# Value products in two pieces instead of three, under a new order of all operations (fused attention and token mixing, one core)

## The chip, the cores and the metric

The kernel runs on one core of a Trainium2 chip. The metric is the device time of one execution in microseconds (us), the median of three runs. Each execution computes the whole problem: eight batches of attention with eight heads each, and behind each batch a mixing stage.

## What is computed

```python
scores = matmul(q, k^T) / sqrt(64)               # (8, 8, 576, 576)
scores = where(scores >= max(scores) - tau, scores, -1e9)
attn = exp(scores - max) ; attn = attn / (sum(attn) + 1e-9)
x = matmul(attn, v)                              # heads side by side: (8, 576, 512)
theta = x @ w_theta
zr, zi = x * cos(theta), x * sin(theta)
u = x + w_tok_r @ zr + w_tok_i @ zi              # mixing along the sequence
out = u + relu(u @ w_ch)
```

All inputs are float32. The large products are made of three products each of rounded high and low parts.

## The kernel before, in words

The work goes by pairs of heads: 8 batches x 4 pairs = 32 pairs, numbered 0 to 31. Everything is kept transposed, with channels on the partitions.

One pair has five units of scores (`unit`, line 743), the first four of 128 queries for each of two heads, the last of 64 queries of both. A unit is one run of score products on TensorE (line 759), then on VectorE an eviction with the row maximum (line 780) and a small addition (line 790), on ScalarE two activations that apply the threshold and the exponential (lines 804 and 811), and on VectorE a transpose in blocks of 32 x 32 (lines 823 and 825) into the tile `a`. There is one buffer of `a` (`n_a` is 1), so the transposes of a pair wait until the value products of the pair before have read it.

When all transposes of a pair are there, `values` (line 829) multiplies with v. These are 18 x 4 x 2 = 288 small products of 32 rows, 64 columns and 144 streamed elements (line 840), which use the array as eight tiles of 32 x 64. Every product is one weight load and one matmul, so a pair has 576 TensorE instructions there. They add up in four banks of PSUM. The 18 steps are cut into `parts` pieces of equal size, each one operation of the plan, and the operations between two pieces may be anything the order puts there:

```python
parts = AT["parts"]
for i in range(parts):
    c0, c1 = 18 * i // parts, 18 * (i + 1) // parts
    pe(..., lambda c0=c0, c1=c1: products(c0, c1), key + A("vs", n) * i, (a, v), (ps,),
       32 * (c1 - c0), mode="w", hold=[x])
```

After them ScalarE copies the four banks to `xT` (lines 853 and 856), and `divide` (line 860) divides by the row sums. After the fourth pair of a batch, `mixture` (line 913) adds the mixing stage: products with w_theta and w_ch (line 948), sine and cosine (lines 1044 to 1051), transposes on TensorE (line 1091) and the products along the sequence (line 1136). All of these are products of 128 rows, 128 columns and 128 to 288 elements, and they are spread over the next batch's four pairs, so that TensorE has them beside the attention. The first pairs have the conversion of the weights beside them (`convert`, line 552).

The order is written out. Every operation of every engine is recorded in a plan with a number; `Plan.run` then issues all of them in one list, `ORDER` (line 144), which holds the differences of the numbers. Each engine works through its own operations in the order of that list, and waits where data or a buffer is not ready. `PLACES` says which buffer or bank each operation uses. Queues of DMAs are issued by SyncE (SP) in the same list.

```python
for word in ORDER.split():
    step, times = (word + "*1").split("*")[:2]
    for _ in range(int(times)):
        n += int(step)
        self.ops[n].fn()
```

Followed through these numbers, the three pieces of a pair stand directly behind one another on TensorE in all 32 pairs: 288 small products in a row, with 126 to 486 other TensorE instructions between one pair's and the next pair's.

Of the kernel before, what the change touches and what calls it, by code (L numbers as in the profile page):

```python
# [64 lines left out]
        "0112101021012012011200120102102010210212021200210221021201021012012100"  # L65
    ),
    "xl": (
        "010320010120001230101201310230123021310231023102301320123201301230123102302130213"
    ),
    "xh": (  # L70
        "01120310032003230210310102310201230113021301230123120310232103102310230123012301230132102310230213"
    ),
    "rb": (
        "010101010010010101010000000000100000001000000100"
    ),
    "bank": (
        "77756745564674655645670000000060000006000000500000064776467564577657653457545746667654564757000000300000"
        "05000000500000056447567455327563476564577677547476760000006000000500000060000005754676754234763654645475"
        "66647554677600000050000006000000500000075475766544237426655665673447656476570000004000000400000050000006"
        "57465764553275656475476534547657466700000070000007000000700000066547566745324536574764567676574567470000"  # L80
        "00700000060000005000000456467547653624754765564577756745656700000060000007000000600007542354736525626275"
        "464625734576735467"
    ),
    "z": (
        "1021212012001200102010201200120010201200101"
    ),
    "rawq": (
        "01100110110101010010110101011110"
    ),
    "q": (  # L90
        "0123012301230123012301230123012301230123012301230123012301230123"
# [11 lines left out]
        "01320123103120132013202103130120132101230120103102110201231032031020132121031012032011032012102130112302"  # L103
        "13210123011201230023102103203123021103202310100210312102301201102302120103201012012131032013233210231300"
        "12301201201010203210310322012302031320101201020110210012310231102321012103201120"
    ),
    "nm": (
        "01010101012010201010200100120101010100100101010012010100101010010010120110101012100100101201010100101001"
        "00101210100010010101020011011201001010010010120101001010"
    ),  # L110
    "s2": (
        "01010010101001201120010100120010212010121001001212102101021201120012011001201012010120101010020100120101"
        "20110120102010210112001021011200112101021010211020101021"
    ),
    "rows": (
        "00010001010100101010101010010100"
# [5 lines left out]
        "01234560123405612340516203452160"  # L122
# [8 lines left out]
        "0102011001320120012010230123010201010123010101230123012001230231"  # L131
    ),
    "zl4": (
        "0123203101320123012332010123201301230123012010230123012301230231"
    ),
    "zh1": (
        "01010101010101000000000100010101"
    ),
    "zl1": (
        "01100101011001100101010100100101"  # L140
# [1172 lines left out]
```

## Time and profile before

| what | value |
|---|---|
| median of three runs | 979.58 us (978.79 to 985.16) |
| profiled execution, its own time | 993.05 us |
| span of the profiled execution | 991.3 us |
| TensorE busy | 885.7 us (89%), 14632 matmuls |
| VectorE busy | 714.8 us (72%) |
| ScalarE busy | 701.1 us (71%) |
| GpSimd busy | 311.9 us (31%) |
| mean granted TensorE clock | 0.96 of full speed |

In the profile, PE is TensorE's matmuls and PEld its weight loads, which run beside them; DVE is VectorE, ACT is ScalarE, POOL is GpSimd, SP is SyncE. "Idle before" a group is the time for which the engine had nothing running just before, with what ended it; "issue" there means that the engine waited for nothing that the profile shows. A matmul in the profile lasts until its modelled end, and the next one starts before that.

### The profile page before, as it was taken

Reading aid. Unit: us, or ns where it says so; the run is one execution under the profiler, and the core shown is the slowest. Engines: PE = TensorE matmul, PEld = TensorE weight load, DVE = VectorE, ACT = ScalarE, POOL = GpSimd, SP = SyncE. Lnnn points to the kernel's source line nnn. Section 1 sums busy time; section 2 is a strip of 40 time slices with the busy share of each in tenths; the row PEclk is TensorE's granted clock in tenths of the full one; section 3 lists DMA queues with packets and bytes.
Section 4 is the critical chain, followed back from the end, with each engine's and each line's share of the span. In section 5 each row is a group of like instructions: output and inputs, shape, how many; then the busy total and the mean of one; then the engine's idle time right before and its main releaser. Section 6 shows DMA issues by size and latency. Waiting matters only on the chain.

```text
span 991.3 us, 34023 instructions
## 1 busy us (share of the span) xinstructions
PE 885.7 (89%) x14632; PEld 799.8 (81%) x14632; DVE 714.8 (72%) x1598; ACT 701.1 (71%) x1406; POOL 311.9 (31%) x390
## 2 busy tenths in 40 slices
PE   5678789988999999988899999998999898998898
PEld 3556678877898888978798888887898887998898
DVE  7889879866778877657777777686777676775343
ACT  6778789755997569845978569865787558974450
POOL 1223425312344325332334323422145221621201
PEclk9788899989999999989999999999999999999899
DMA  6446453444613354223603344315342343224301
GB/s 240 127 146 200 147 172 119 127 154 136 205 61 121 125 165 163 86 88 93 236 9 142 121 162 150 119 42 174 116 152 76 108 151 120 87 95 134 114 34 69
DMA packets 62375, 126.15 MB, mean 127 GB/s; under 512 B 22512, under 2 KB 31632, under 8 KB 58128
## 3 DMA queue, kind: packets, MB, share of 16 engines
q1 hardware_dynamic: 62080, 123.97, 37.7%
q8 instruction: 115, 1.88, 0.8%
q14 instruction: 36, 0.29, 0.1%
q10 hardware_dynamic: 144, 0.00, 0.0%
HBM read 110.17 MB, written 13.78 MB: 125 GB/s over the span
## 4 chain that ended last, share of the span: by engine, by line
PE 69%; DVE 17%; issue 9%; ACT 3%; POOL 0%; DMA 0%; DVEq 0%; ACTq 0%; POOLq 0%
PE banks_ps__66 L1136 20%; PE banks_ps__66 L840 17%; PE banks_ps__66 L948 15%; PE banks_ps__66 L759 12%; DVE sc L780 7%; DVE a L823 4%; PE banks_ps__66 L1091 3%; DVE nm L790 1%; PE banks_ps__66 L634 1%; ACT sc L804 1%; ACT s L811 1%; DVE xl L530 1%; PE banks_ps__66 L871 1%; DVE xT L1197 0%; DVE a L825 0%
## 5 line engine op out<-in xcount | busy, mean ns | idle before, releaser
L804 ACT ACTIVATE sc<-sc,nm 128x576 f32<-128x576 f32 x288 | 217.4, 772 | 88.8 <-DVE nm L790 88.4
L823 DVE STREAM_TRANSPOSE a<-s 128x576 f32<-128x576 f32 x256 | 190.0, 759 | 123.1 <-PE banks_ps__66 L840 110.3
L840 PE MATMUL banks_ps__66<-a,v 32*64 32x144 f32 x9216 | 175.1, 296 | 62.8 <-issue 61.6
L811 ACT ACTIVATE s<-sc,small 128x576 f32<-128x576 f32 x288 | 223.0, 775 | 7.1 <-DVE a L823 2.4
L840 PEld LDWEIGHTS banks_ps__66<-a,v 32*64 32x64 f32 x9216 | 155.6, 136 | 79.0 <-issue 73.2
L780 DVE TENSOR_SCALAR_CACHE_REDUCE sc<-banks_ps__66 128x576 f32<-128x576 f32 x261 | 187.1, 744 | 44.0 <-PE banks_ps__66 L759 41.5
L759 PE MATMUL banks_ps__66<-k,q 64*128 64x288 f32 (+1 forms) x1728 | 180.7, 322 | 24.6 <-DVE sc L780 16.5
L759 PEld LDWEIGHTS banks_ps__66<-k,q 64*128 64x128 f32 (+1 forms) x1728 | 142.8, 197 | 51.3 <-DVE sc L780 26.5
L948 PE MATMUL banks_ps__66<-xh,wm 128*128 128x288 f32 x1024 | 173.2, 309 | 3.4 <-issue 2.8
L1136 PE MATMUL banks_ps__66<-wt_h,zh 128*128 128x288 f32 x576 | 163.0, 307 | 2.1 <-ACT zh L1097 1.7
L1136 PE MATMUL banks_ps__66<-wt_l,zh 128*128 128x288 f32 x576 | 161.6, 303 | 0.0
L948 PEld LDWEIGHTS banks_ps__66<-xh,wm 128*128 128x128 f32 x1024 | 147.8, 194 | 14.6 <-issue 11.9
L1066 POOL TENSOR_TENSOR z<-z,xT 128x288 f32<-128x288 f32 x112 | 91.3, 847 | 105.3 <-ACT z L1047 105.3
L1136 PEld LDWEIGHTS banks_ps__66<-wt_h,zh 128*128 128x128 f32 x576 | 109.5, 191 | 5.0 <-ACT zh L1097 2.1
L1136 PEld LDWEIGHTS banks_ps__66<-wt_l,zh 128*128 128x128 f32 x576 | 109.7, 191 | 2.1 <-issue 1.9
L530 POOL TENSOR_TENSOR xl<-xT,xh 128x288 fp32r<-128x288 f32 x78 | 65.1, 855 | 131.1 <-ACT xh L907 74.4
L1136 PE MATMUL banks_ps__66<-wt_h,zl 128*128 128x288 f32 x576 | 97.8, 305 | 1.1 <-DVE zl L1116 1.1
L530 POOL TENSOR_TENSOR k<-rawk,k 128x288 fp32r<-128x288 f32 x62 | 53.3, 872 | 135.9 <-ACT k L724 56.1
L948 PE MATMUL banks_ps__66<-xl,wm 128*128 128x288 f32 x512 | 92.5, 303 | 0.7 <-POOL xl L530 0.6
L853 ACT COPY xT<-banks_ps__66 128x512 f32<-128x512 f32 x32 | 18.8, 586 | 103.8 <-PE banks_ps__66 L840 103.8
L1136 PEld LDWEIGHTS banks_ps__66<-wt_h,zl 128*128 128x128 f32 x576 | 82.5, 190 | 4.3 <-issue 2.7
L894 POOL TENSOR_TENSOR xT<-xT,rb 128x288 f32<-128x288 f32 x48 | 39.4, 836 | 139.0 <-ACT xT L853 87.3
(78 smaller groups left out, 1068.1 us busy)
## 6 DMA issues: line engine op xcount, KB each, us to landing
v<-in_vp_dram SPq DMA_DIRECT2D x32, 1152.0 KB
wm<-wm_dram SPq DMA_DIRECT2D x64, 512.0 KB
rawq<-in_qT_dram SPq DMA_DIRECT2D x31, 320.0 KB
rawk<-in_kT_dram SPq DMA_DIRECT2D x31, 288.0 KB
out_dram<-xT SPq DMA_DIRECT2D x31, 288.0 KB
rb<-sums_dram SPq DMA_DIRECT2D x64, 128.0 KB
z<-in_w_tok_dram SPq DMA_DIRECT2D x9, 576.0 KB
wm_dram<-rb SPq DMA_DIRECT2D x16, 256.0 KB
```

The costliest lines, as they stand in the source:

```text
L530: eng.tensor_tensor(out=out()[:, c0:c1], in0=in0()[:, c0:c1], in1=in1()[:, c0:c1], op=ALU.subtract)
L759: nc.tensor.matmul(ps()[:, 2 * j + h, :HS], q[a]()[r, i * P : (i + 1) * P], k[c]()[r, h * HS : (h + 1) * HS], start=(x == 0), stop=(x == 2),)
L780: lambda j=j, sc=sc, scaled=scaled: nc.vector.tensor_scalar(out=sc().rearrange("p (a b) -> p a b", a=2), in0=ps()[:, 2 * j : 2 * j + 2, :H ...
L804: lambda j=j, sc=sc: nc.scalar.activation(out=sc(), in_=sc(), func=AF.Prelu, bias=nm()[:, 2 + j : 3 + j], scale=-1.0, alpha=STEEP),
L811: lambda j=j, sc=sc, total=total, weights=weights: nc.scalar.activation(out=weights(), in_=keys(sc()), func=AF.Exp, bias=back, accum_out=p ...
L823: nc.vector.transpose(out=a()[:, :, j, 32 * i : 32 * i + 32], in_=src.rearrange("p (c q) -> p c q", q=32))
L840: nc.tensor.matmul(ps()[64 * h : 64 * h + 64, b, :w], v()[r, c, h, :], a()[r, c, h, :], start=(c == 0), stop=(c == 17))
L894: eng.tensor_tensor(out=x()[:, r], in0=x()[:, r], in1=rc()[:, r], op=ALU.mult)
L948: nc.tensor.matmul(ps[h]()[:, :HS], wm()[:, a, c, :], parts[c][bb]()[:, h * HS : (h + 1) * HS], start=first and n == 0, stop=final and n = ...
L1066: eng.tensor_tensor(out=zi, in0=zi, in1=x[m]()[:, c0:c1], op=ALU.mult)
L1091: nc.tensor.transpose(out=tp()[:, i * P : (i + 1) * P], in_=z()[:, c : c + P], identity=ident)
L1136: nc.tensor.matmul(ps()[:, :HS], zz[c][lo]()[:, zz[c][2]], w[:, c, hs], start=(q + n == 0), stop=(q + n == len(work) - 1),)
```

## The change

`parts` becomes 2: each pair's value products are two operations of 144 small products (288 TensorE instructions each) in place of three of 96. The plan has 4369 operations in place of 4401, as many instructions on each engine's data path as before (14632 matmuls), and a new `ORDER` and new `PLACES`. All other numbers of `AT`, the buffers and the functions stay.

```diff
-    "px0": 2, "pu0": 2, "lc": 1, "ka": 4, "vq": 1, "pd": 3, "vs": -2.88, "parts": 3, "ab": 0, "sq": 3, "acc": 0.1,
+    "px0": 2, "pu0": 2, "lc": 1, "ka": 4, "vq": 1, "pd": 3, "vs": -2.88, "parts": 2, "ab": 0, "sq": 3, "acc": 0.1,
...
 ORDER = (
-    "176 -176 177 1 1 -9 10 1 -10 1*4 8 1 1 44 1 -44 45 -230 1*3 189 2 -1 -7 2 -184 183 44 -36 37 2 -1 -44 9 -2 1 5 "
...
+    "176 -176 179 -2 1 2 -10 1 1 9 -8 1 1 54 -46 2 -1 46 -44 1 44 -38 1 -5 6 1 36 1 1 -46 3 -1 13 2 -1 31 -38 -5 7 "
...
```

Followed through the new numbers, the two pieces of a pair no longer stand together. Between them stand, in the order of the pairs, 10, 16, 18, 24, 114, 50, 44, 40, 40, 54, 44, 40, 40, 68, 44, 50, 40, 54, 44, 40, 48, 52, 42, 40, 32, 120, 56, 48, 50, 54, 44 and 48 other TensorE instructions (median 44). From pair 4 on all of them belong to products and transposes of 128 rows of the mixing stage, to the one transpose of `divide`, or (pairs 5 and 6) to the conversion of w_ch. In pairs 0 to 3 they are the transpose of `divide` and products of the conversion. On the other engines the positions of most operations have moved as well.

## Rows read from the trace of the kernel before

**Rows 1.** The page's part 1: busy time, share of the span, instructions of each engine.
```profile
PE 885.7 (89%) x14632; PEld 799.8 (81%) x14632; DVE 714.8 (72%) x1598; ACT 701.1 (71%) x1406; POOL 311.9 (31%) x390
```
**Rows 2.** The page's part 4: the chain that ended last, by engine.
```profile
PE 69%; DVE 17%; issue 9%; ACT 3%; POOL 0%; DMA 0%; DVEq 0%; ACTq 0%; POOLq 0%
```
**Rows 3.** Waits of PE: what it waited for, us in total, times, longest.
```profile
PE banks_ps__66 L840 <- issue: 61.6, 37, 4.0
PE banks_ps__66 L759 <- DVE sc L780: 16.5, 18, 1.8
PE banks_ps__66 L759 <- DVE q L705: 6.1, 1, 6.1
PE banks_ps__66 L871 <- DVE rows L867: 4.0, 4, 2.1
```
**Rows 4.** Timeline of PE around one pair: start, length, what, [idle before].
```profile
629.74 0.69 PE L1136 MATMUL banks_ps__66<-wt_h,zl 128*128 128x288 f32 x4
630.36 2.51 PE L840 MATMUL banks_ps__66<-a,v 32*64 32x144 f32 x144
633.57 2.27 PE L840 MATMUL banks_ps__66<-a,v 32*64 32x144 f32 x128 [0.70 <-issue]
637.04 0.51 PE L840 MATMUL banks_ps__66<-a,v 32*64 32x144 f32 x16 [1.20 <-issue]
```
**Rows 5.** Timeline of PE around another pair, and the products behind it.
```profile
318.86 3.00 PE L840 MATMUL banks_ps__66<-a,v 32*64 32x144 f32 x176
322.73 2.02 PE L840 MATMUL banks_ps__66<-a,v 32*64 32x144 f32 x112 [0.87 <-issue]
324.68 0.40 PE L1136 MATMUL banks_ps__66<-wt_h,zh 128*128 128x288 f32 x1
...
325.18 0.30 PE L1136 MATMUL banks_ps__66<-wt_l,zh 128*128 128x288 f32 x1
325.31 0.29 PE L1136 MATMUL banks_ps__66<-wt_h,zh 128*128 128x288 f32 x1
```
**Rows 6.** The page's part 3: instruction packets by queue.
```profile
q8 instruction: 115, 1.88, 0.8%
```
**Rows 7.** Timeline of PE's weight loads around the pair of rows 5.
```profile
318.86 2.73 PEld L840 LDWEIGHTS banks_ps__66<-a,v 32*64 32x64 f32 x176 [0.16 <-issue]
...
324.68 0.19 PEld L1136 LDWEIGHTS banks_ps__66<-wt_h,zh 128*128 128x128 f32 x1 [0.20 <-issue]
```
**Rows 8.** Line 840 by itself: duration in ns, min/median/max.
```profile
L840 PE MATMUL banks_ps__66<-a,v x9216: 277/281/498, 29.0 to 920.6; 32*64 32x144 f32 x197
L840 PEldq EVENT_SEMAPHORE  x31: 51/51/51, 53.6 to 909.5; - x31
```
**Rows 9.** Waits of VectorE and ScalarE for the value products.
```profile
DVE a L823 <- PE banks_ps__66 L840: 110.3, 22, 9.1
ACT xT L853 <- PE banks_ps__66 L840: 103.8, 31, 11.4
```
**Rows 10.** Stretches: length, busy PE PEld DVE ACT POOL, PEclk, DMA share, GB/s.
```profile
30.00:180.00 150.00, 125.08 (x2048) 104.04 (x2035) 129.11 (x264) 121.03 (x247) 54.30 (x69) 0.89 0.48 152
180.00:620.00 440.00, 405.49 (x7150) 369.56 (x7149) 322.88 (x737) 323.71 (x654) 145.43 (x176) 0.98 0.39 131
620.00:910.00 290.00, 266.70 (x4579) 243.98 (x4578) 206.33 (x474) 212.10 (x424) 95.84 (x118) 0.98 0.34 113
```
**Rows 11.** Timeline of VectorE around the pair of rows 5.
```profile
320.27 0.55 DVE L696 TENSOR_SCALAR rawq<-rawq,small 128x640 f32<-128x640 f32 x1
324.88 0.78 DVE L823 STREAM_TRANSPOSE a<-s 128x576 f32<-128x576 f32 x1 [4.07 <-PE banks_ps__66 L840]
```

More of the change, by code (lines that the diff above doesn't have):

```diff
@@ L64 @@
     "wm": (
-        "0112101021012012011200120102102010210212021200210221021201021012012100"
+        "0101201220220101200012012001201201201201022100121010210210012012011200"
     ),
     "xl": (
-        "010320010120001230101201310230123021310231023102301320123201301230123102302130213"
+        "012102012001010231010120303120123201301230213012310230123301210232013102310232013"
     ),
     "xh": (
-        "01120310032003230210310102310201230113021301230123120310232103102310230123012301230132102310230213"
+        "01203121013003013120120213201323010103210310230123210301230213012312030123102310231023102320131023"
@@ L72 @@
     ),
     "rb": (
-        "010101010010010101010000000000100000001000000100"
+        "010101010001010101010000001000100000011101010100"
     ),
     "bank": (
-        "77756745564674655645670000000060000006000000500000064776467564577657653457545746667654564757000000300000"
-        "05000000500000056447567455327563476564577677547476760000006000000500000060000005754676754234763654645475"
-        "66647554677600000050000006000000500000075475766544237426655665673447656476570000004000000400000050000006"
@@ L80 @@
-        "57465764553275656475476534547657466700000070000007000000700000066547566745324536574764567676574567470000"
-        "00700000060000005000000456467547653624754765564577756745656700000060000007000000600007542354736525626275"
-        "464625734576735467"
+        "67765674454565747576560000000070000007000000700000074567545744744475677457667547667576477675000000600000"
+        "06000000600000056547646757456744754665674747677564570000005000000700000060000004765476576574567747655567"
+        "74476545675600000040000007000000600000077564757467556437476556747564674775670000006000000600000070000006"
@@ L83 @@
+        "65745576564654776746554766575647745600000040000004000000600000047456567465556774564574677546754765760000"
+        "00300000070000007000000576457675457467357456654767676476547600000060000006000000500005573273654727244354"
+        "663726656457766453"
     ),
     "z": (
-        "1021212012001200102010201200120010201200101"
+        "1201010212001200120012001200120012001200101"
     ),
     "rawq": (
-        "01100110110101010010110101011110"
+        "01011100110010100101101010100010"
@@ L89 @@
     ),
     "q": (
-        "0123012301230123012301230123012301230123012301230123012301230123"
+        "0123012301302103120312031203120312031203120312031201320123012301"
     ),
@@ L102 @@
     "sc": (
-        "01320123103120132013202103130120132101230120103102110201231032031020132121031012032011032012102130112302"
-        "13210123011201230023102103203123021103202310100210312102301201102302120103201012012131032013233210231300"
-        "12301201201010203210310322012302031320101201020110210012310231102321012103201120"
+        "10231032013201230132100231032101023031201230231202031012030112031021012020120123021032110213201230120310"
+        "13202130012303102130120321103201203012302130023103201320120312231020123012313210103202103121032031023102"
+        "31010230012301320132030123201301230130210230120301231123021031203121031321020310"
     ),
     "nm": (
-        "01010101012010201010200100120101010100100101010012010100101010010010120110101012100100101201010100101001"
-        "00101210100010010101020011011201001010010010120101001010"
+        "01010101010101020010100101001010101010100101010101201001001010001010012001010010100102010201010100101001"
+        "00102010010200100101001102100102001010010010120101010010"
     ),
     "s2": (
-        "01010010101001201120010100120010212010121001001212102101021201120012011001201012010120101010020100120101"
-        "20110120102010210112001021011200112101021010211020101021"
+        "01010010100101010010012101020201010100120112001001102010101010210001011020101102010100101010001100121010"
+        "10120210010011201001001102100101002001102012011001001102"
     ),
     "rows": (
-        "00010001010100101010101010010100"
+        "00100001001000101001010101000000"
     ),
@@ L121 @@
     "xT": (
-        "01234560123405612340516203452160"
+        "01234560321405632140536410253461"
     ),
@@ L130 @@
     "zh4": (
-        "0102011001320120012010230123010201010123010101230123012001230231"
+        "0120012001020132012301320102102001021023101001010102020101010101"
     ),
     "zl4": (
-        "0123203101320123012332010123201301230123012010230123012301230231"
+        "0123012001320132012301320132102001321023102301200123023101230120"
     ),
     "zh1": (
-        "01010101010101000000000100010101"
+        "01010010000100100001000100010101"
     ),
     "zl1": (
-        "01100101011001100101010100100101"
+        "01010101010101100101000101010101"
     ),
```

260 rows, old and new, of the table ORDER are left out of this document.

## The prediction

> **What bounds the kernel now.** I read the page's busy times first: TensorE is busy for 885.7 of 991.3 us, VectorE and ScalarE for some 72% [rows 1]. So the time is TensorE's work plus what it idles, about 105 us. The chain that ended last says the same: 69% on TensorE, and 9% "issue", time in which an engine waited for nothing that the profile shows [rows 2]. The waits of TensorE name that item: 61.6 of its idle microseconds stand before small value products of line 840, in 37 pieces of 1.66 us on average, and no semaphore ended them. The waits for other engines are much smaller, 16.5 us for score evictions and single digits below that [rows 3].
>
> What the engine lacks there is seen in the timeline. In one pair 144 value products run, then comes a gap, then exactly 128, a gap, then 16 [rows 4]; in another 176, a gap, and 112 [rows 5]. A product is a load and a matmul, so 128 products are 256 instructions. I counted every instruction of TensorE's queue, with the waits that stand as instructions of their own (line 840 has 31 [rows 8]): all 37 stalls begin at places whole multiples of 256 apart. The instruction queue with 115 packets moved 1.88 MB [rows 6], which is 16 KB a packet, and 29,264 products and loads [rows 1] over 115 are 254. So instructions come in blocks of 256, and TensorE stands still where it has eaten a block before the next has come.
>
> It can do so only in value products. The 144 of rows 4 took 2.51 us less the 0.28 that the last one's own length adds [rows 8], 16 ns each: a block of 128 lasts 2.05 us. A product of the mixing stage starts 0.13 us after the one before it (325.18 to 325.31 [rows 5]): a block of those lasts 17 us. From the first stall's end to the second's in rows 4 are 3.47 us, nearly all of it waiting for one block to come. What a stall really takes is its idle time and also what the last product's modelled end hides, 0.28 less 0.02: 1.92 us on average, 71 us for all 37. So a block takes about 2.05 + 1.92 = 4.0 us to come, with a spread: the longest idle is 4.0 us [rows 3], which makes some 6.3 us.
>
> **The change, part by part.** The number of products, their kind and their operands stay. What changes on TensorE is what lies between the pieces. Before, 576 instructions of value products stood in a row, and nearly every pair had one block, and some two, with nothing else in it. Now two runs of 288 have mostly 40 to 54 others between them, nearly all products of 128 columns. A block that holds the whole gap has 20 broad products of 0.133 us and 108 small ones of 16 ns, 2.7 + 1.7 = 4.4 us, and a little for the switches: enough for the next block to come. A block that lies inside one run of 288 still has nothing else and stalls as before.
>
> Which blocks these are follows from the new order, with the block bounds where the stalls of before put them and the extra wait instructions as dense as before (about 4.6 a pair). In the same count the old order has 39 blocks of value products alone. The new one has 5 to 10 (as the bounds shift by some instructions), 9 to 16 with 238 to 255 value instructions, and 8 to 14 with 222 to 237.
>
> *Stalls.* Removed: 37 x 1.92 = 71 us. Left: 8 full blocks at 1.92 = 15 us. A block of the middle kind has 122 small and 6 broad products, 1.95 + 0.8 and a switch of 0.2, so 3.0 us against 4.0: I take 0.9 for 13 of them, 12 us. Between nothing, where the next block was already on its way, and 2 us, where it is late, this is the term with the widest ends. The third kind lasts about 3.7 us; in the trace of before seven such blocks lost little, 0.16 us on average: 2 us. Together 29 us are left, and 42 us go.
>
> *Switches.* Value products use the array as tiles of 32 x 64, the others as a whole. Going in and coming out leaves the weight loads idle for 0.16 and 0.20 us [rows 7], 0.36 together. By the starts of matmuls it is 0.3: the first broad one behind a run comes some 0.2 us after the last small one instead of 16 ns [rows 5], and the first small one 0.1 later than a broad one would. The cut adds one such excursion to each of 32 pairs: 32 x 0.3 = 9 us on TensorE's own path, where nothing hides it. Above: 32 x 0.36 = 12. Below: nothing, where the engine would have stood anyway; a gain is excluded, since the broad products ran before without these switches between them.
>
> The Trainium skill, in "TensorEngine Tiling (Array Packing)", Key Properties, says that changing the tiling mode drains TensorE. This speaks against the cut; if each of the two switches drained one product's whole 0.28 us [rows 8], 32 x 0.56 = 18 us would be added and the forecast would be 9 us later. The idle of rows 7 is smaller, so I stay with the rows.
>
> *The early stretch.* From 30 to 180 us VectorE is busy for 129.1 of 150 us [rows 10], with the conversion of the weights beside the attention. There a TensorE that stalls less mostly waits for VectorE instead. Five of the stalls lie there, some 10 us; I give half of it back, 5 us. Later VectorE is busy for 323 of 440 and 206 of 290 us [rows 10], and TensorE can use what it wins.
>
> *Other engines.* The tile `a` has one buffer, and VectorE's transposes of the next pair wait for the last value product: 110.3 us in 22 waits [rows 9], 4.07 us in the pair of rows 5 [rows 11]. From the first to the last value product a pair takes now 288 x 16 ns and 71/32 of stall, 6.8 us. With the cut it is 4.6 + 0.9 of stall + 2.7 of products between + 0.3 of switch = 8.5 us. VectorE waits some 1.7 us longer in each pair, 54 us in all; it has 276 us idle [rows 1], of which this takes 164, and ScalarE's copy of the sums [rows 9] comes as much later. I cost this at nothing: the cover is VectorE's remaining 112 us. The other moved operations, among them loads on SP's queue and GpSimd's subtractions, I also put at nothing, since I see no side on which they err: their ends are the other waits of rows 3, some 30 us that could shrink by a third or grow by a third, 10 us either way.
>
> *Sum.* -71 + 29 + 9 + 5 = -28 us. The profiled execution took 993.05 us (span 991.3) and should come to 965. It is 1.4% above the median of 979.58; the terms scale by that to less than half a microsecond, so the median goes to 952 us. A difference of under 1%, some 10 us, is about what a measurement of this kernel can't tell from none.
>
> **The rivals.** *The supply keeps pace everywhere.* If the bounds fall as the new order wants them, so that every block has a dozen or more broad products, only some 5 us of stalls are left: -71 + 5 + 9 + 5 = -52, 928 us. For it: blocks with up to 237 value instructions hardly stalled before. Against it: my count leaves 5 to 10 full blocks wherever I put the bounds.
>
> *The stalls move rather than go.* A block that comes later because DMAs of loads are ahead of it takes up to 6.3 us, and a mixed block of 4.4 us doesn't cover that. If most of the gaps are too short, 45 us are left, the switches cost 12 and the early stretch gives back all 10: -71 + 45 + 12 + 10 = -4, 976 us. For it: the spread of the stalls up to 4.0 us [rows 3]. Against it: the first stall of rows 4 is 0.70 us only, so many blocks come in 3 us.
>
> *The wait for `a` becomes the loop (slower).* Place: the transposes of line 823 behind the last value product. If the time from the end of one pair's values to the start of the next pair's is set by VectorE and ScalarE, then each pair lasts longer by the 1.7 us that the values are spread over: 54 us, less half of the 42 us of stalls that shorten it elsewhere: about 1012 us. It decides from the point at which VectorE's idle time outside this wait, 5.2 us a pair (276 - 110 over 32), is used up. For it: 17% of the chain runs over VectorE [rows 2]. Against it: 1.7 is a third of 5.2.
>
> **How the numbers follow.** The forecast, 940 to 965 us, gets 0.58. The first rival, 920 to 940, gets 0.20. The second, 965 to 985, gets 0.16, half of it above 970. The slower one gets 0.06. Faster by over 1% (below 969.8): 0.58 + 0.20 + 0.08 = 0.86; within 1%: 0.08 and a little of the last, 0.09; slower: 0.05. The range takes in the first rival nearly whole and the second up to its sum: 926 to 974.
>
> **What would show it.** In the profile after: idle of TensorE before line 840 with "issue" falls from 61.6 us to 20 to 30, in 12 to 22 pieces; each pair's timeline shows 144 value products, 5 to 60 others, 144 again, and where a gap is left, it cuts a run inside one piece. The weight loads show the switches of 0.16 and 0.20 us twice in a pair. VectorE's wait at line 823 grows by some 50 us without TensorE waiting for line 823 or 780 for more than 10 us longer. The prediction is wrong if the gaps stay at 40 us or more, if they vanish, or if the idle time turns up again before lines 759, 948 and 1136.

## The result, and the profile after

The changed kernel takes 927.5 us (median of four runs, 924.78 to 931.48) against 981.63 for the kernel before in the same comparison: a ratio of 0.945 with a 95% interval of 0.9395 to 0.9505. That is 54 us, nearly twice the 28 forecast, and just above the 926 where the range began. The profiled execution took 924.78 us (span 923.0, before 991.3).

The page's part 1 and, from part 4, the chain by engine, of the kernel after, as in [rows 1] and [rows 2]:

```profile
PE 866.0 (94%) x14632; PEld 779.5 (84%) x14632; DVE 714.4 (77%) x1598; ACT 699.5 (76%) x1406; POOL 314.3 (34%) x390
...
PE 64%; DVE 20%; ACT 8%; issue 3%; DMA 3%; POOL 1%; SPq 0%; DVEq 0%; POOLq 0%; ACTq 0%
```

The same instructions are there; "issue" fell from 9% of the chain to 3%. The waits of TensorE, as in [rows 3]:

```profile
PE banks_ps__66 L759 <- DVE sc L780: 24.0, 25, 2.5
PE banks_ps__66 L759 <- DVE q L705: 5.8, 1, 5.8
PE banks_ps__66 L948 <- issue: 4.2, 3, 2.7
...
PE banks_ps__66 L840 <- issue: 0.8, 1, 0.8
```

What stood first with 61.6 us in 37 pieces is 0.8 us in one. All "issue" rows of this view together fell from 64.9 to 6.1 us, while all waits for other engines rose from 36.3 to 46.3. The timeline of TensorE around pair 10, the pair of [rows 5]:

```profile
302.75 2.51 PE L840 MATMUL banks_ps__66<-a,v 32*64 32x144 f32 x144
305.19 0.28 PE L871 MATMUL banks_ps__66<-ident,rows 128*9 128x128 f32 x1
305.22 0.38 PE L1136 MATMUL banks_ps__66<-wt_h,zh 128*128 128x288 f32 x1
...
306.10 0.95 PE L948 MATMUL banks_ps__66<-xh,wm 128*128 128x288 f32 x6
306.90 1.35 PE L1136 MATMUL banks_ps__66<-wt_h,zl 128*128 128x288 f32 x9
308.18 2.51 PE L840 MATMUL banks_ps__66<-a,v 32*64 32x144 f32 x144
310.62 1.06 PE L948 MATMUL banks_ps__66<-xh,wm 128*128 128x288 f32 x6
```

Two whole runs of 144 in 2.51 us each, broad products between them, and no gap anywhere. The weight loads show the price, the switches into and out of the small tiles, now twice in a pair:

```profile
302.74 2.24 PEld L840 LDWEIGHTS banks_ps__66<-a,v 32*64 32x64 f32 x144 [0.16 <-DVE sc L780]
305.18 0.09 PEld L871 LDWEIGHTS banks_ps__66<-ident,rows 128*9 128x9 f32 x1 [0.20 <-issue]
...
308.18 2.24 PEld L840 LDWEIGHTS banks_ps__66<-a,v 32*64 32x64 f32 x144 [0.16 <-issue]
310.62 0.83 PEld L948 LDWEIGHTS banks_ps__66<-xh,wm 128*128 128x128 f32 x6 [0.20 <-issue]
```

A second difference stands in the granted clock. Stretches of the kernel after, with the columns of [rows 10]:

```profile
30.00:180.00 150.00, 128.79 (x2371) 106.00 (x2359) 134.94 (x287) 130.05 (x267) 54.52 (x72) 0.94 0.51 161
180.00:620.00 440.00, 430.46 (x7523) 391.19 (x7522) 348.50 (x788) 348.67 (x702) 164.84 (x197) 1.00 0.40 136
620.00:850.00 230.00, 224.45 (x3912) 204.97 (x3918) 179.38 (x411) 177.62 (x359) 80.62 (x98) 1.00 0.39 130
```

From 180 us on the clock is at its upper level (2.4 GHz) for all but 3.4 us, where it was 0.98 before [rows 10]. What made the difference is seen around the longest stall of the kernel before, again in stretches (the last one stands behind another stall):

```profile
205.40:208.40 3.00, 3.00 (x195) 3.00 (x196) 1.98 (x6) 2.80 (x5) 0.00 (x0) 1.00 0.80 292
208.80:212.70 3.90, 0.00 (x0) 0.00 (x0) 0.00 (x0) 1.51 (x3) 0.00 (x0) 0.81 0.43 141
212.80:217.80 5.00, 5.00 (x102) 4.34 (x103) 1.72 (x3) 0.83 (x3) 0.00 (x0) 0.50 0.02 4
218.20:224.00 5.80, 5.80 (x52) 5.31 (x51) 4.90 (x14) 2.31 (x4) 0.00 (x0) 1.00 0.91 304
834.30:840.00 5.70, 5.70 (x131) 5.13 (x131) 1.47 (x5) 3.79 (x8) 0.14 (x1) 1.00 0.03 7
```

At 1.00 the engine works through small products, then it stands still for 3.9 us, and the 5 us behind the stall run at 0.50, the lower level of 1.2 GHz. Such a stall is paid twice. All eight stretches of the lower clock between 180 and 910 us begin in a stall or within 1.6 us behind one. But not every long stall is followed by one: the last line stands behind 3.20 us of idle time, and the clock stays at 1.00. Over the whole span the mean clock rose from 0.959 to 0.989: at half speed for (1 - 0.959) x 2 x 991 = 81 us before, and for 20 us after.

### The profile page after: what moved, and what is told of

The parts are those of the page before. It is cut to its first block, busy times and chain, and to the rows that moved or that the text cites. A ratio compares the mean times of both kernels' runs of the same rounds, so it can differ in the third digit from the quotient of the medians.

```text
span 923.0 us, 34024 instructions
## 1 busy us (share of the span) xinstructions
PE 866.0 (94%) x14632; PEld 779.5 (84%) x14632; DVE 714.4 (77%) x1598; ACT 699.5 (76%) x1406; POOL 314.3 (34%) x390
## 4 chain that ended last, share of the span: by engine, by line
PE 64%; DVE 20%; ACT 8%; issue 3%; DMA 3%; POOL 1%; SPq 0%; DVEq 0%; POOLq 0%; ACTq 0%
PE banks_ps__66 L1136 21%; PE banks_ps__66 L840 14%; PE banks_ps__66 L948 13%; PE banks_ps__66 L759 11%; DVE sc L780 7%; DVE a L823 5%; PE banks_ps__66 L1091 3%; ACT sc L804 2%; ACT s L811 2%; DVE nm L790 1%; PE banks_ps__66 L634 1%; DMA z<-in_w_theta_dram 1%; DVE xl L530 1%; DVE z L1016 1%; DVE zl L1116 1%
## 5 line engine op out<-in xcount | busy, mean ns | idle before, releaser
L759 PE MATMUL banks_ps__66<-k,q 64*128 64x288 f32 (+1 forms) x1728 | 178.7, 320 | 32.7 <-DVE sc L780 24.0
L948 PE MATMUL banks_ps__66<-xh,wm 128*128 128x288 f32 x1024 | 168.9, 302 | 4.2 <-issue 1.6
L840 PE MATMUL banks_ps__66<-a,v 32*64 32x144 f32 x9216 | 165.0, 288 | 4.9 <-DVE sc L780 3.9
L840 PEld LDWEIGHTS banks_ps__66<-a,v 32*64 32x64 f32 x9216 | 146.9, 132 | 18.0 <-issue 9.2
L948 PEld LDWEIGHTS banks_ps__66<-xh,wm 128*128 128x128 f32 x1024 | 143.4, 188 | 14.6 <-issue 8.6
L1136 PE MATMUL banks_ps__66<-wt_h,zl 128*128 128x288 f32 x576 | 95.8, 301 | 0.0
L1116 DVE TENSOR_TENSOR zl<-banks_ps__66,zh 128x512 fp32r<-128x512 f32 (+1 forms) x96 | 51.9, 547 | 56.1 <-ACT zh L1097 56.0
L1136 PEld LDWEIGHTS banks_ps__66<-wt_h,zl 128*128 128x128 f32 x576 | 81.5, 188 | 2.9 <-issue 2.4
L948 PEld LDWEIGHTS banks_ps__66<-xl,wm 128*128 128x128 f32 x512 | 75.0, 188 | 7.1 <-issue 6.0
```

The source lines that it names most:

```text
L759: nc.tensor.matmul(ps()[:, 2 * j + h, :HS], q[a]()[r, i * P : (i + 1) * P], k[c]()[r, h * HS : (h + 1) * HS], start=(x == 0), stop=(x == 2),)
L840: nc.tensor.matmul(ps()[64 * h : 64 * h + 64, b, :w], v()[r, c, h, :], a()[r, c, h, :], start=(c == 0), stop=(c == 17))
L948: nc.tensor.matmul(ps[h]()[:, :HS], wm()[:, a, c, :], parts[c][bb]()[:, h * HS : (h + 1) * HS], start=first and n == 0, stop=final and n = ...
L1116: lambda zh=zh, zl=zl, tv=tv: nc.vector.tensor_tensor(out=zl(), in0=tv(), in1=zh().bitcast(F32), op=ALU.subtract),
L1136: nc.tensor.matmul(ps()[:, :HS], zz[c][lo]()[:, zz[c][2]], w[:, c, hs], start=(q + n == 0), stop=(q + n == len(work) - 1),)
```

## The experiments

My theory was that the gap between the pieces feeds the instruction queue and that this is the gain. The main rival was that the rest of the new order is. All kernels but one keep the computation and move instructions; one adds transposes whose result nothing reads. In the sketches V is a run of value products, and x are the broad products that stand between or beside them on TensorE. The kernel before was measured again beside each set of runs, and the ratios are to that.

| kernel | median us | ratio to before | PE "issue" us | PE other waits us |
|---|---|---|---|---|
| before | 981.6 to 988.5 | 1 | 64.9 | 36.3 |
| after | 927.5 | 0.945 | 6.1 | 46.3 |
| new order, joined early | 1018.4 | 1.033 | 49.9 | 78.3 |
| new order, joined late | 1032.4 | 1.046 | 51.8 | 81.5 |
| new order, cut at 13 of 18 steps | 963.2 | 0.975 | 27.4 | 48.2 |
| new order, bounds shifted | 929.9 | 0.942 | 8.2 | 38.0 |
| new order, four pieces | 958.5 | 0.971 | 3.3 | 55.1 |
| new order, gap 64 | 978.4 | 0.990 | 11.9 | 74.3 |
| new order, gap 32 | 969.7 | 0.986 | 8.8 | 70.6 |
| new order, gap 20 | 976.2 | 0.992 | 14.2 | 72.1 |
| old order, gap 40 | 1011.7 | 1.025 | 10.5 | 99.0 |
| old order, gap 24 | 985.6 | 0.999 | 14.8 | 74.1 |
| the same, joined early | 1033.4 | 1.047 | 56.0 | 70.2 |
| the same, joined late | 1031.6 | 1.048 | 55.0 | 77.3 |

The last two columns are the sums of all rows of the view of TensorE's waits, those that say "issue" and those that name an engine or a DMA. The ratios' intervals reach 0.002 to 0.008 to either side.

**The gap taken away from the new order.** Second piece moved up:

```diff
-V1 x x x x x V2
+V1 V2 x x x x x
```

> The changed kernel with the second value piece of every pair moved up to stand directly behind the first; everything else keeps the new order. Theory (the gap between the pieces feeds the instruction queue): some 37 stalls of about 1.9 us come back where 7 are left now, 58 us, less 32 switches of 0.3 us, 10 us, and the granted clock falls again behind the long stalls: 975 to 995 us, issue idle before line 840 near 60 us. Rival (the rest of the new order is worth the time, the gap little): 930 to 945 us.

Measured: 1018.35 us, ratio 1.0331 (1.0255 to 1.0408). The waits of this kernel (its list of the order takes two more lines, so line 842 is line 840 of the others):

```profile
PE banks_ps__66 L842 <- issue: 48.2, 39, 2.9
PE banks_ps__66 L761 <- DVE sc L782: 27.1, 27, 2.2
PE banks_ps__66 L761 <- ACT xT L858: 12.2, 9, 3.5
PE banks_ps__66 L950 <- DVE xT L1199: 6.1, 5, 2.8
```

The stalls are back, 39 of them, as the theory wants. But the kernel is 91 us slower than the changed one and slower than the one before, beyond what I gave either side: waits for other engines also rose, from 46 to 78 us. Joined the other way:

```diff
-V1 x x x x x V2
+x x x x x V1 V2
```

> The changed kernel with the first value piece of every pair moved down to stand directly ahead of the second. Supply theory: about as many stalls at block bounds as in the first joined kernel (41, 64 us), and so 927 + 53 for stalls + some 19 for the lower clock - 10 for switches = 990 us. If the further time that the first joined kernel took came from the broad products being out of place behind the values, and not from the second piece standing early: also here 1010 to 1020 us.

Measured: 1032.35 us, ratio 1.0459 (1.0401 to 1.0516). So the extra does not come from the second piece standing early. The new order without its gap is worse than the old one.

**The gap put into the old order.** The kernel before, two pieces, products of the neighbourhood moved between them:

```diff
-"parts": 3
+"parts": 2
...
-x x x V1 V2 V3 x x x
+x V1 x x x x V2 x
```

> The kernel before with its value products cut into two pieces and broad products of its own neighbourhood moved between them: 40 to 44 instructions in 25 of the pairs, 0 to 32 in seven; all other operations keep the old order. Theory: some 28 stalls of 1.9 us go, 53 us, and some 28 switches of 0.3 us come, 8 us: 925 to 945 us. Rival (the new order's other moves are needed, above all because the tile a is held longer): 960 us or more, with VectorE's wait at line 823 well above 110 us.

Measured: 1011.71 us, ratio 1.0251 (1.0199 to 1.0304). The stalls went as expected and the time did not. The rival that I gave has the time right and its sign wrong: VectorE's wait for the value products at line 823 is 102 us here, not well above 110. The waits (line 841 is line 840 of the others, and so on by one):

```profile
PE banks_ps__66 L760 <- DVE sc L781: 27.8, 39, 2.1
PE banks_ps__66 L760 <- ACT xT L857: 14.4, 16, 2.5
PE banks_ps__66 L841 <- DVE sc L781: 14.1, 17, 2.0
PE banks_ps__66 L841 <- issue: 9.6, 11, 1.8
PE banks_ps__66 L841 <- DVE a L824: 8.8, 6, 3.8
```

Against [rows 3], "issue" fell from 61.6 to 9.6 us, and score units now wait for the banks of the value sums (line 857) and value products for score evictions and transposes. All waits for other engines rose from 36 to 99 us. With a smaller gap:

```diff
-x x V1 V2 V3 x x
+x V1 x x V2 x
```

> The kernel before with two value pieces and a gap of at most 24 to 26 TensorE instructions, taken only from the broad products between the values and the nearest score unit on either side; 24 pairs get 20 or more. Theory (the products in the gap are taken from the filling between the score units, so the price goes with their number): stalls fall to 15 or fewer, and with half the products moved half of the price: 960 to 985 us. Rival (any cut costs this order the same, because a and the four banks are held longer): 1000 us or more, as with the gap of 40.

Measured: 985.63 us, ratio 0.9985 (0.9959 to 1.001): no difference from the kernel before, just over the upper end of what I gave. So the gap alone bought the old order nothing. That left two readings: the gap's own price ate the gain, or it is dear in itself to let products change places with value pieces. Two kernels tell them apart. They keep the new places of the small-gap kernel and only join the pieces (in the traces every other operation has the same order on its engine):

```diff
-x V1 x x V2 x
+x V1 V2 x x x
```

> The kernel with the old order and the small gap, with every second piece moved up directly behind the first: the same broad products have changed places with value products as there, but there is no gap. If changing places costs by itself in the old order, and the gap won back there what it cost: stalls as in the kernel before (39, 78 us) and 1025 to 1045 us. If the changed places cost nothing and the gap's own price (switches, a and the banks held longer) ate what it won: 980 to 990 us.

```diff
-x V1 x x V2 x
+x x x V1 V2 x
```

> The same with the first piece moved down directly ahead of the second. As for the early one: 1025 to 1045 us if changed places cost by themselves, 980 to 990 us if the gap's own price ate the gain.

Measured: 1033.38 us, ratio 1.0471 (1.0434 to 1.0507), and 1031.62 us, ratio 1.0482 (1.043 to 1.0534). One row of the waits of the early one, then the same of the small gap:

```profile
PE banks_ps__66 L840 <- issue: 51.1, 35, 4.0
```

```profile
PE banks_ps__66 L840 <- issue: 13.3, 13, 3.5
```

With the uneven cut below this is the clearest reading of the study. At equal places the gap takes 4.9% off, 1.047 to 0.9985, some 48 us, and it does so through "issue". Other waits are the same with it and without (74.1 against 70.2 and 77.3 us). What ate the gain in the old order was the changed places, which cost about as much, 46 us, with no gap at all.

**How much of a run is too much.** The changed kernel with the cut after 13 of 18 steps, everything else in place:

```diff
-c0, c1 = 18 * i // parts, 18 * (i + 1) // parts
+c0, c1 = (0, 13, 18)[i], (0, 13, 18)[i + 1]
```

> The changed kernel with the cut after 13 of the 18 steps in place of 9: 208 and 80 products, at the same places in the order. Theory: a run of 416 instructions holds a whole block in about 20 of the pairs, so about 20 stalls of 1.9 us: 38 us more, 960 to 970 us, and less than joined. Rival (what counts is that something stands between the pieces, or that VectorE and ScalarE get work there): 925 to 932 us.

Measured: 963.2 us, ratio 0.9753 (0.9698 to 0.9808), as the theory gave. TensorE's timeline in pair 23:

```profile
670.98 2.66 PE L840 MATMUL banks_ps__66<-a,v 32*64 32x144 f32 x146
675.92 1.26 PE L840 MATMUL banks_ps__66<-a,v 32*64 32x144 f32 x62 [2.28 <-issue]
677.11 1.33 PE L948 MATMUL banks_ps__66<-xl,wm 128*128 128x288 f32 x4
```

The run of 208 stops after 146, and the run of 80 behind the gap does not. No operation changed its place, and other waits hardly moved (48.2 against 46.3 us), so the price of a stall can be read here. The stalls at block bounds take 34.2 us from start to start against 10.5 in the changed kernel, 23.7 more. The mean clock fell from 0.989 to 0.977, by the rule above 44 us at half speed against 20, and half of the 24 us more is 12. Together 35.7 us; the medians differ by 35.7. That these agree to the tenth is luck: the profiled executions differ by 40.5 us, and the ratios by 0.030, some 30 us.

**Where the bounds fall.** 64 transposes ahead of everything:

```diff
+for _ in range(64):
+    nc.tensor.transpose(out=psum[:, 7, :P], in_=ident, identity=ident)
 plan.run()
```

> The changed kernel with 64 transposes of the identity (128 instructions, at 0.11 us each some 7 us) at the head of TensorE's queue, so that all block bounds fall 128 instructions earlier in the order. If a block is asked for about 61 instructions before it is needed to begin, no window of 317 instructions is value products alone and 10 or fewer stalls come wherever the bounds fall: 927 to 936 us. If only whole blocks of 256 count: 5 to 10 blocks stall by 1.9 us more: 945 us.

Measured: 929.88 us, ratio 0.9415 (0.9363 to 0.9466). With all bounds moved by half a block the time is that of the changed kernel, so the gain does not hang on lucky bounds.

```profile
PE banks_ps__66 L840 <- issue: 4.6, 6, 1.6
```

**Other gaps and more pieces.** Four pieces in place of two:

```diff
-V1 x x x x x V2 x
+V1a x V1b x x x x V2a x V2b
```

> The changed kernel with each of its two pieces cut once more and one broad operation of 2 to 8 instructions put into 51 of the 64 cuts. If a switch of the array costs 0.3 us on the path: 51 x 0.3 = 15 us more, 942 us. If the switches are hidden: 927 us. If the shorter runs take the stalls that are left (7, some 11 us) and the switches are hidden: 916 us.

Measured: 958.49 us, ratio 0.9706 (0.9651 to 0.9762), 31 us over the changed kernel for 51 cuts, 0.6 us each, and above all three that I gave. The timeline has the price of a switch by itself (line 845 is line 840 of the others, line 953 is line 948):

```profile
225.69 1.65 PE L845 MATMUL banks_ps__66<-a,v 32*64 32x144 f32 x64
227.26 0.80 PE L953 MATMUL banks_ps__66<-xh,wm 128*128 128x288 f32 x4
227.99 1.29 PE L845 MATMUL banks_ps__66<-a,v 32*64 32x144 f32 x64
```

The last small product of the first line starts 0.28 us before its end, at 227.06, and the next small one 0.93 us later. Four broad products at 0.133 us and one small one would take 0.55, so the way into the broad products and back costs 0.38 us; the median of all such cuts is 0.39. For 51 cuts that is 20 us, and other waits rose by 9, together 29 of the 31. A wider gap, and two narrower ones in which only the second piece moves up:

> The changed kernel with the gap between the pieces widened to about 64 instructions from pair 5 on, by neighbouring broad products. If the stalls that are left (6, 10 us) go and the moved products cost nothing: 915 to 920 us. If the moved products are missed elsewhere, as in the old order: 935 to 950 us.

> The changed kernel with every second piece moved up until 20 to 26 TensorE instructions are left between the pieces (10 to 18 in the first three pairs). Supply theory: a window of 317 instructions still holds 24 or more that are not value products, about 4.2 us with the switches, so nearly as few stalls as with the full gap (6 to 12): from the supply alone 927 to 935 us. If products that change places with a value piece are missed where the new order had them, whatever the supply does: half of the 28 us that joining cost beyond stalls, clock and switches, 940 to 950 us.

> The same with 32 to 36 instructions left, some 10 fewer than in the new order for most pairs. Supply theory: as many stalls as in the changed kernel, 925 to 932 us. If the new order's places matter as such: between the changed kernel and the one with 20, 932 to 940 us.

Measured: 978.39 us for 64 (ratio 0.9895, 0.9859 to 0.993), 976.19 us for 20 (0.9917, 0.9883 to 0.9951), 969.69 us for 32 (0.9859, 0.9789 to 0.9929). All three keep "issue" low, and all three lose most of the 54 us. The kernel with 32 is the sharpest case: second pieces moved past some five products, stalls at block bounds of 13.4 us against 10.5, and 42 us more. Its waits:

```profile
PE banks_ps__66 L759 <- DVE sc L780: 26.1, 26, 2.5
PE banks_ps__66 L948 <- DVE xT L1197: 6.4, 5, 2.8
...
PE banks_ps__66 L948 <- DVE xh L909: 5.4, 4, 2.1
```

More products now reach TensorE before a bank is evicted (line 1197) or their rounded operand is there (line 909); no single row carries the loss. By the pages TensorE idles 84.0 us there and 57.0 in the changed kernel, and is busy for 886.4 us against 866.0, at a mean clock of 0.975 against 0.989: waits and the lower clock share the loss. Both my theories were too mild here: the price of a place is not in proportion to how far an operation moves. No kernel that I made was faster than the changed one beyond the intervals.

## Why the prediction was right, and where its size was off

The side, the mechanism and the place were right; the size was half. The 927.5 us lie inside the range by 1.5 us, and only because the range took in the first rival. One of the prediction's own signs of being wrong also came: the gaps before line 840 all but vanished, 0.8 us where 20 to 30 were forecast. By its steps:

- **Stalls.** That value products outrun instruction blocks of 256 and that the gap feeds the queue held in every kernel, and a stall took 1.6 to 2.0 us on average. The term of what is left was mis-sized: "8 full blocks at 1.92 = 15 us", 12 and 2, together 29 us. Measured are six gaps over 0.6 us at block bounds, 10.5 us from start to start, against 78.1 before. By kinds, the two of full blocks or nearly full ones took 3.4 us, the two of the middle kind 4.5 and the two of the third 2.6. The count of blocks was nearly right: five blocks of the changed kernel hold value products alone. But only one of them stalled, by 1.06 us. The step that failed is "a block that lies inside one run of 288 still has nothing else and stalls as before".

  The records of the instruction queue's packets in the traces show what happens in its place. In the kernel before, TensorE goes on 1.2 to 1.8 us after a packet of 16 KB has landed, at each of the 37 stalls, and that packet had started only after the block ahead had begun, up to 4.0 us after. In the changed kernel all six gaps end so, 1.2 to 1.5 us after a landing, also the two (2.3 and 1.3 us of idle time) that the view of waits puts to GpSimd and ScalarE. Of its five full blocks, the one that stalled had the next block's packet start 0.45 us after it had begun; for the other four the packet started 0.28 to 2.29 us before. So the next block is asked for somewhat ahead, and where slower instructions stand ahead of a block of value products, this buys the time that the block itself lacks. The shifted kernel fits that: three of its six full blocks stalled, those whose packets started 0.57 to 1.51 us after them, and the other three, whose packets started before them, did not stall by more than 0.45 us.

  How far ahead in instructions is not shown. The kernel file has the constants `BLOCK = 256` and `AHEAD = 61`, which nothing in it uses; counted over a block and the 61 instructions ahead of it, every window of the kernel after lasts at least some 4.2 us, while some 31 of the kernel before last less than 3.6. That fits, but no run varied the 61. The first rival, all blocks fed, with its 928 us, was the better forecast, by a mechanism that I didn't see; that it is right to 1 us is luck, since it has no term for the clock either.
- **The clock.** I had no term for it. From 180 to 910 us the kernel before spent (1 - 0.98) x 2 x 730 = 29 us at the lower level [rows 10] (34 by the clock's own records), the one after 3.4. Broad products start 133 ns apart at 1.00 and 240 ns at 0.50 there, small ones 16 and 30 ns, so where TensorE sets the pace about half of that time is lost, an estimate of some 15 us. The uneven cut shows the same coupling with nothing else moved.
- **Switches.** The weight loads idle for 0.16 and 0.20 us, twice in a pair, as forecast. By starts of matmuls an excursion costs 0.38 to 0.39 us (four pieces), not 0.3, since the second broad product also starts late (in pair 10 at 305.44 us, 0.22 us behind the first in place of 0.13); 32 of them are 12 us, the upper end that I gave, where the sum has 9 (32 x 0.3 is 9.6). It is less than the 0.56 us, 18 us in all, that draining for a whole product's length would give.
- **The early stretch.** "I give half of it back, 5 us" was wrong in direction: pair 5 starts its values at 165.40 us where they started at 183.59, 18 us earlier, more than the stalls there. Which part of the new order did that I didn't try.
- **Other engines.** I costed the longer hold of `a` at nothing, which held, but expected VectorE's wait at line 823 to grow by some 50 us. Against that sign it fell, from 110.3 us [rows 9] to

```profile
DVE a L823 <- PE banks_ps__66 L840: 28.6, 18, 5.4
```

  From the first to the last value product of a pair it did get longer, 7.1 to 8.4 us on average. The wait depends on what VectorE's list has ahead of the transposes, which the new order changed. The rival with this wait as the loop did not come about. The other waits of TensorE grew by 10 us, the end of what I allowed them.

Sum of the profiled executions: stalls 10.5 - 78.1 = -68, clock -15, switches +12, other waits +10: -61 us, of -68 (993.05 to 924.78). It is an estimate; the two gaps named above, 3.6 us of idle time, stand in it as stalls and as other waits. The pages divide the same 68 us otherwise: TensorE idles 57.0 us where it idled 105.6, and is busy for 866.0 where it was 885.7. The profiled execution of before was 11 us above the median, so the medians differ by less, 54.

What stays open: what the rest of the new order is worth. Changed places cost 42 to 51 us in the new order (gaps of 32, 20 and 64; up to 10 us of stalls are in it) and some 46 in the old one, the gap is worth about 48 at equal places in the old order, and the new order without its gap is 30 to 45 us slower than the old one. So I read the 54 us as the gap in an order whose places were fitted to it; what that fitting would give without the stalls was not tried.

## What to carry to other kernels

When an engine idles with no releaser, count its instructions between the idle places: equal distances (here 256) suggest that it waits for its own code, which the landings of the instruction queue's packets can confirm, and short instructions in long runs are where to look. Cut such runs and put slower instructions that are ready between the pieces: here blocks filled by runs of 288 instructions ended in two stalls, those of 416 (uneven cut) in 19 and those of 576 in 37. In an order that is balanced instruction by instruction, weigh a cut against a control with the same places and no cut; here the cut alone looked worthless (0.9985) and was worth 4.9%.

## What the runs showed of the hardware

Blocks of instructions came 2.8 to 6.3 us after the block before them had begun, 4.0 on average over the 37 stalls. The spread lies in when the packet starts, 0.0 to 4.0 us after that block has begun; once it has landed, 1.2 to 1.8 us pass until TensorE goes on. What makes a packet start late was not tried. At the longest stall, where it started 4.0 us late, the DMA engines had been busy to 0.80 just before (first line of the stretches above).

The Trainium skill, in "Advanced Engine Details and Errata", ISA Cache, gives lines of 16 KB or 256 instructions and says there are only two; the trace agrees with the 16 KB and the 256 [rows 4, rows 6]. It also names 128 KB for TensorE, which would be eight such lines, an estimate from its figures. Eight lines fetched ahead would have held the 576 instructions of a pair, so the 37 stalls speak against that many being fetched ahead; how many are kept no run here shows.

The lower clock behind a stall was not expected: 3.9 us of standing still, then 5 us at 0.50; elsewhere 3.20 us of standing still, then 1.00. In the kernel after, from 180 to 850 us, 655 of 670 us are busy and the clock is 1.00.
